# Turning softmax weights on VectorE and ScalarE in place of TensorE, for two pairs of every unit

## The chip, the cores and the metric

The kernel runs on one core of a Trainium2 chip. A core has five engines that run side by side, each through its own list of instructions in order: TensorE (PE, matmuls; its weight loads are shown apart as PEld), VectorE (DVE), ScalarE (ACT), GpSimd (POOL) and SyncE (SP), which issues the transfers (DMA) between DRAM and the on-chip memory SBUF. Matmul results land in eight banks of a second on-chip memory, PSUM. They meet by semaphores. The metric is the device time of one execution, in microseconds (us).

## The reference

Attention inside chunks of 64 positions, and a feed-forward layer behind it, all in float32:

```python
scores = scale * np.matmul(q_c, k_c.transpose(0, 1, 2, 4, 3))     # (8, 8, 9, 64, 64)
scores = scores - np.max(scores, axis=-1, keepdims=True)
attn = np.exp(scores)
attn = attn / (np.sum(attn, axis=-1, keepdims=True) + 1e-09)
out = np.matmul(attn, v_c)
...
x = np.ascontiguousarray(attn_out.transpose(0, 2, 1, 3)).reshape(B, S, H * D)   # 8 x 576 x 512
xn = (x - mu) / np.sqrt(var + 1e-06) * g_ln
ch = np.maximum(xn @ w_ch1, 0.0) @ w_ch2          # 512 to 2048 to 512
return x + ch
```

## The kernel before

The 4608 rows are cut into 18 pairs of 256 rows; nine tiles hold two pairs each. The first three tiles are done by a starting part, in which the weights are also converted. The other six make three units of two tiles, or four pairs. A unit's feed-forward part (`unit_ffn`) is a long row of matmuls on TensorE, in a form with seven products in place of eight. While unit u runs on TensorE, the attention of the four pairs of unit u + 1 is woven in between: so in unit 0 and in unit 1, not in unit 2, and four times in all for the pairs in question (second and fourth).

What sets the order is a table. `attention` is a generator: each `yield` ends a step. `weave` lets the unit's matmuls count a cost (6 for a step of six matmuls, in lines L1109) and runs the next step of a pair once the count reaches the pair's begin (`BEGINS`) plus the step's number in its table (`PAIR_STEPS`). The order on each engine is fixed by this when the program is built; nothing is moved at run time.

The steps of one of these pairs: load q and k; scores by 64 small matmuls (L326); maximum along a row (L333, `top`); scores minus maximum (L359) into `p_sb`, whose 128 partitions hold two chunks' queries and whose 1024 columns hold eight pairs of heads' keys; exponential on ScalarE (L362); the transposed weights `pt_sb`; row sums and their reciprocal (L405 to L407); weights times V (L427); division by the sum (L461); statistics of the rows; normalization on ScalarE (L493); a turn (L500) and sixteen transfers into `rows` (L508), from which `combine` (L811 to L826) builds the next unit's operands in the later part of the unit.

The transposed weights come in three ways. `by_pe` is used in the starting part. In the units, the first and third pair (`STEPS`, `WIDE`) turn 32 x 256 blocks across partitions by sixteen VectorE instructions (L398). The second and fourth (`BY_TENSOR`, `AT_END`) do eight 128 x 128 transposes on TensorE into PSUM (L386) and two copies out by ScalarE (L389).

Beside this ScalarE and VectorE serve the unit's own matmuls. A quarter of the first layer (`q`, 14 steps of six matmuls) uses four PSUM banks, two `a` and two `c`; products with different names accumulate in the same bank one after another, so a copy of a bank's state to `snap` (L1115) or its addition to `hu` (L1118) must be done before the bank is written again: two steps later for the copies of the second and fourth step (index 1 and 3), three or four for the others.

Of the kernel before, what the change touches and what calls it, by code (L numbers as in the profile page):

```python
# [8 lines left out]
F32 = mybir.dt.float32  # L9
# [5 lines left out]
ALU = mybir.AluOpType  # L15
AX = mybir.AxisListType

P = 128
# [7 lines left out]
HP = H // 2  # L26
# [9 lines left out]
LEAD = 3  # L36
# [14 lines left out]

BEGINS = (4, 92, 154, 240)
STEPS = (0, 5, 9, 14, 20, 31, 42, 53, 61, 67, 72, 77, 85, 90, 97, 104, 116, 128, 140)
BY_TENSOR = (-20.9, 6, 11, 18, 33, 37, 40, 48, 54, 60, 67, 72, 80, 86, 98, 110, 122)
WIDE = (-13.9, 5, 9, 14, 22, 35, 48, 61, 69, 75, 80, 85, 93, 98, 105, 110, 122, 134, 146)
AT_END = (-10.9, 6, 11, 18, 33, 37, 40, 48, 54, 62, 72, 77, 84, 92, 104, 116, 128)
PAIR_STEPS = (STEPS, BY_TENSOR, WIDE, AT_END)
SUMS = (392, 402, 414, 545, 563, 578, 590, 602, 604, 616, 628, 640, 658.5, 664, 674)
LATE = (4, 12, 76, 82, 88, 96, 104, 112)
MIXING = ((8, 10, 14, 18, 40, 48, 50, 64), (64, 66, 70, 74, 84, 92, 94, 108))  # L60
# [41 lines left out]
def quad(i):  # L102
    return slice(32 * i, 32 * i + 32)
# [3 lines left out]
def chunk_attention_ffn(ctx: ExitStack, tc: tile.TileContext, qkv, v01, g, g_col, w, out):  # L107
    nc = tc.nc
# [7 lines left out]
    small = ctx.enter_context(tc.tile_pool(name="small", bufs=4))  # L116
# [9 lines left out]
    ident = const.tile([P, P], F32, name="ident")  # L126
# [137 lines left out]
    def sums(pair):  # L264

        if pair not in ys:
            ys[pair] = [ps_y.tile([P, DM], F32, name="y") for _ in range(2)]
        return ys[pair]
# [9 lines left out]
        nc.sync.dma_start(x, spilled[pair])  # L278
        return x

    def attention(pair, xt_cols, xs, by_pe, den_by_pe, rows_of=None, pt_raw=False, pt_by_pe=False):

        moved = pair >= 2 * LEAD + 4
        if pair == 1:
# [13 lines left out]
        groups = 2 * HP  # L298

        def banks():  # L300
            return ps_a.tile([P, 2, DM], F32, name="s")

        def rows(bank):
            return bank.rearrange("p (a d) -> p a d", d=D)

        def halves():

            if den_by_pe:
                assert pair not in taken
                return sums(pair)  # L310
            both = banks()
            return [both[:, j, :] for j in range(2)]
# [7 lines left out]
        for j in range(2):  # L320
            for a in range(HP):
                for h2 in range(2):
                    r = slice(h2 * D, (h2 + 1) * D)
                    for c in range(2):
                        cs = slice(j * P + c * D, j * P + (c + 1) * D)
# [22 lines left out]
        p_sb = work.tile([P, groups, 2, D], F32, name="p_sb", tag="work")  # L348
# [16 lines left out]
        if den_by_pe:  # L365
            nc.gpsimd.memset(v_1.rearrange("p j a b d -> p (j a b) d")[:, :, D:], 1.0)

        if pt_raw:
            pt_sb = raws.tile([P, groups, 2, D], F32, name="pt_raw", tag="wf")
        else:  # L370
            pt_sb = work.tile([P, groups, 2, D], F32, name="pt_sb", tag="work")
        if by_pe:
            pt = halves()
            for a in range(groups):
                cs = slice(a % HP * P, (a % HP + 1) * P)
                nc.tensor.transpose(out=pt[a // HP][:, cs], in_=p_sb[:, a, :, :], identity=ident)  # L376
            for j in range(2):
                nc.scalar.copy(
                    pt_sb[:, j * HP : (j + 1) * HP], pt[j].rearrange("p (a c t) -> p a c t", a=HP, c=2)
                )  # L380
            yield
        elif pt_by_pe:
            pt = halves()
            for a in range(groups):
                cs = slice(a % HP * P, (a % HP + 1) * P)
                nc.tensor.transpose(out=pt[a // HP][:, cs], in_=p_sb[:, a, :, :], identity=ident)  # L386
            yield
            for j in range(2):
                nc.scalar.copy(  # L389
                    pt_sb[:, j * HP : (j + 1) * HP], pt[j].rearrange("p (a c t) -> p a c t", a=HP, c=2)  # L390
                )
            yield
        else:
            for h2 in range(2):
                for j in range(2):
                    for c in range(2):
                        for i in range(2):
                            nc.vector.transpose(  # L398
                                out=pt_sb[quad(2 * h2 + j), :, c, quad(i)], in_=p_sb[quad(2 * c + i), :, h2, quad(j)]
                            )  # L400
                    yield
        den = small.tile([P, groups, 2], F32, name="den")
        rden = small.tile([P, groups, 2], F32, name="rden")
        if not den_by_pe:
            nc.vector.tensor_reduce(out=den, in_=p_sb, axis=AX.X, op=ALU.add)  # L405
            nc.vector.tensor_scalar_add(den, den, 1e-9)
            nc.vector.reciprocal(rden, den)  # L407
            yield

        if by_pe:  # L410
# [9 lines left out]
        for j in range(2):  # L420
            for a in range(HP):
                for h2 in range(2):
                    r = slice(h2 * D, (h2 + 1) * D)
                    ja = j * HP + a
                    for c in range(2):
                        cs = slice(c * D, (c + 1) * D)
# [13 lines left out]
        if den_by_pe:  # L440
# [3 lines left out]
                out=x_j[:, 0], in0=o4[:, :, :, :D], in1=r_b[:, :, :HP].broadcast_to([P, 2, HP, D]), op=ALU.mult  # L444
            )
            for h2 in range(2):
                nc.vector.tensor_tensor(
                    out=x_j[:, 1, h2], in0=o_j[1][h2][:, :, :D], in1=r_b[:, h2, HP:].broadcast_to([P, HP, D]),
                    op=ALU.mult,
                )  # L450
            taken.remove(pair)
        elif by_pe:
            nc.vector.tensor_tensor(
                out=x.rearrange("p j (a b d) -> p b (j a) d", a=HP, b=2),
# [3 lines left out]
        else:  # L458
            x_h = x.rearrange("p j (a b d) -> p (j a) b d", a=HP, b=2)
            for h2 in range(2):  # L460
                nc.vector.tensor_tensor(  # L461
                    out=x_h[:, :, h2, :], in0=rows(o[h2]),
# [22 lines left out]
        if not rows_of:  # L485
            for j in range(2):
                nc.vector.scalar_tensor_tensor(
                    out=xg[:, j, :], in0=x[:, j, :], scalar=mv[:, j, 0:1], in1=g_sb, op0=ALU.subtract, op1=ALU.mult
# [9 lines left out]
        if rows_of and moved:  # L498
            turned = keep.tile([P, 4, 2 * NK, 32], F32, name="x")
            nc.vector.transpose(  # L500
                out=turned.rearrange("p b a t -> p a b t"),
                in_=xg.rearrange("p j (k b f) -> p (j k) b f", k=NK, b=4),
# [281 lines left out]
    def rows_of(i):  # L784
        if "rows" not in shared:
            shared["rows"] = [xtp.tile([P, 2, 2, NK, P], F32, name="rows", tag=f"xt{c}") for c in "hl"]
        return shared["rows"][i // 2][:, i % 2]
# [423 lines left out]
    def play(order, streams):  # L1211
        for c in order:
            next(streams[c])

    xs = {}

    class Tokens:
# [7 lines left out]
                self.x.extend(xtp.tile([P, NK, 2 * PAIR], F32R, name=f"xt{c}") for c in "hl")  # L1225
            return [x[:, :, i * PAIR : (i + n) * PAIR] for x in self.x]

        def attention(self, i, by_pe=False, den_by_pe=False, pt_raw=False, pt_by_pe=False):
            rows = None
            if self.t >= LEAD:  # L1230
                rows = lambda: rows_of((self.t - LEAD) % 2 * 2 + i)
            return attention(2 * self.t + i, lambda: self.cols(i), xs, by_pe, den_by_pe, rows, pt_raw, pt_by_pe)

        def ffn(self, i, n, f0=0, f1=NF, room=()):
            first = 2 * self.t + i
# [2 lines left out]
    tiles = [Tokens(t) for t in range(NTILE)]  # L1238
# [8 lines left out]
    with tc.manual_schedule():  # L1247
        nc.scalar.activation(minus, ident, AF.Copy, scale=-1.0)
        play(START, now)
        now.update(  # L1250
            A=now.pop("E"), B=tiles[2].attention(1), C=tiles[3].attention(0, True), D=tiles[4].attention(0, True),
            G=tiles[3].attention(1), H=tiles[4].attention(1, True, pt_raw=True), S=prepare(), R=start_ring(), T=mix(4, nc.gpsimd, const, "w4"),
            U=mix(5, nc.gpsimd, raws, "raw"), V=mix(6, nc.gpsimd, const, "w8"), a=mix(1, nc.vector, const, "w0"),
            b=mix(2, nc.gpsimd, const, "w1"), c=mix(0, nc.vector, const, "w9", True), d=mix(3, nc.gpsimd, const, "w10", True),
            X=bring(range(2 * LEAD - 2, 2 * LEAD)), P=combine(0, 0), Q=combine(0, 1),
        )
        now.update(zip("u1", tiles[1].ffn(0, 2, room=ROOMS[1])))
        play(layout(ROOMS[1], SECOND), now)
        streams = {}

        def following(u, n):
            n, u = n % 4, u + n // 4
            if (u, n) not in streams and u < UNITS:
                by_pe = len(PAIR_STEPS[n]) == len(BY_TENSOR)
                streams[u, n] = tiles[LEAD + 2 * u + n % 2].attention(n // 2, pt_by_pe=by_pe)
            return streams.get((u, n), iter(" "))

        now["N"] = following(1, 0)
        now.update(zip("u1", tiles[2].ffn(0, 2, room=ROOMS[2])))
        play(layout(ROOMS[2], THIRD, True), now)  # L1270
        side = [(at, now["Q"]) for at in REST]
        for stream, steps in zip((now["d"], mix(NF // 2 - 1, nc.gpsimd, const, "w13")), MIXING):
            side += [(at, stream) for at in steps]
        for u in range(UNITS):
            if u + 1 < UNITS:
                for n in range(4):
                    begin, steps = BEGINS[n], PAIR_STEPS[n]
                    side += [(begin + at, following(u + 1, n)) for at in steps]
                    side.append((begin + steps[0] if n < 3 else NEXT, following(u + 1, n + 1)))
                stream = combine(u + 1)  # L1280
                side += [(at, stream) for at in SUMS]
            side = weave(unit_ffn(u), side)
            if u + 1 < UNITS:
                side += [(at, ending[-1]) for at in LATE]
        assert not side
# [38 lines left out]
```

## Time and profile before

| what | value |
|---|---|
| median of three runs | 819.97 us (817.36 to 820.20) |
| profiled execution, its own time | 818.67 us |
| its span | 816.9 us |
| TensorE busy | 806.0 us, 99% of the span |
| VectorE busy | 609.6 us, 75% |
| ScalarE busy | 363.1 us, 44% |
| GpSimd busy | 183.0 us, 22% |

The span is what the profiler saw between the first and the last instruction; 1.8 us of the execution lie around it. A row such as `357.70 1.09 PE s L386 x8` in the chain means: at 357.70 us eight instructions of line 386 began that write the tile `s`, and 1.09 us passed on the chain. In order of time a row gives start, time until its last instruction ended, engine, line, operation, output <- inputs, shapes, how many, and in brackets the idle time ahead of it and what ended that. Neighbours on VectorE and ScalarE can overlap by some hundredths.

### The profile page before, as it was taken

How to read it: one execution, taken by the hardware profiler on the slowest of the kernel's cores; microseconds unless marked ns; L12 is line 12 of the kernel's file. 1: busy time of each engine (PE TensorE's matmuls, PEld its weight loads, DVE VectorE, ACT ScalarE, POOL GpSimd, SP SyncE). 2: the span in 40 equal slices, each digit the busy share in tenths (PEclk: the TensorE clock that was granted, in tenths of full speed). 3: DMA queues.
4: the chain of work that ended last, by engine and by line, in shares of the span. 5: the costliest groups of instructions: out<-in, count | busy, mean ns of one | idle time of the engine just before them, and what ended most of it. 6: DMA issues, size and time to landing. Idle time of an engine off the chain costs nothing.

```text
span 816.9 us, 15499 instructions
## 1 busy us (share of the span) xinstructions
PE 806.0 (99%) x6170; PEld 680.3 (83%) x6170; DVE 609.6 (75%) x885; ACT 363.1 (44%) x545; POOL 183.0 (22%) x199
## 2 busy tenths in 40 slices
PE   7999999999999999999999999999999999999998
PEld 4888888888888888888888898888888988888887
DVE  6999975787665876869789987697799922249974
ACT  4776432121335434344567442443675522345450
POOL 0111005653857975610100001300000040000000
PEclk9999999999999999999999999999999999999999
DMA  9998315967786239988789578877796678668663
GB/s 359 331 291 243 156 52 183 364 201 253 272 307 252 104 129 367 368 300 302 250 248 329 184 236 307 278 276 257 239 334 213 183 236 252 186 203 285 193 214 108
DMA packets 113928, 201.06 MB, mean 246 GB/s; under 512 B 8512, under 2 KB 75072, under 8 KB 109888
## 3 DMA queue, kind: packets, MB, share of 16 engines
q1 hardware_dynamic: 112560, 195.35, 70.2%
q0 software_dynamic: 1296, 4.72, 3.0%
q8 instruction: 49, 0.80, 0.4%
q14 instruction: 23, 0.19, 0.1%
HBM read 142.89 MB, written 48.23 MB: 234 GB/s over the span
## 4 chain that ended last, share of the span: by engine, by line
PE 98%; DMA 1%; DVE 0%; issue 0%; SPq 0%; ACT 0%
PE y L1109 28%; PE h L589 16%; PE y L613 16%; PE y L1039 12%; PE h L1039 10%; PE s L1039 7%; PE s L326 2%; PE h L427 1%; DMA qk<-qkv 1%; PE s L427 1%; PE s L376 1%; PE s L353 0%; PE s L386 0%; PE y L251 0%; PE s L521 0%; PE y L542 0%
## 5 line engine op out<-in xcount | busy, mean ns | idle before, releaser
L1109 PE MATMUL y<-xc,ring 128*128 128x512 f32 x1008 | 233.4, 391 | 0.0
L1109 PEld LDWEIGHTS y<-xc,ring 128*128 128x128 f32 x1008 | 188.0, 188 | 39.5 <-issue 0.4
L613 PE MATMUL y<-wp,hidden 128*128 128x512 f32 x564 | 137.8, 393 | 0.0
L589 PE MATMUL h<-xth,wp 128*128 128x512 f32 (+1 forms) x432 | 129.6, 371 | 0.0
L613 PEld LDWEIGHTS y<-wp,hidden 128*128 128x128 f32 x564 | 104.4, 188 | 21.4
L1118 DVE TENSOR_TENSOR hu<-y,snap 128x512 f32<-128x512 f32 x72 | 49.2, 685 | 78.7 <-ACT snap L1115 38.3
L589 PEld LDWEIGHTS h<-xth,wp 128*128 128x128 f32 x432 | 78.2, 188 | 14.6 <-DVE hidden L603 0.6
L1039 PE MATMUL y<-ring,hx 128*128 128x512 f32 (+1 forms) x448 | 79.8, 337 | 0.0
L1115 ACT COPY snap<-y 128x512 f32<-128x512 f32 x72 | 41.8, 587 | 83.9 <-PE y L1109 83.8
L935 ACT ACTIVATE hx<-hu 128x1024 fp32r<-128x1024 f32 x61 | 64.3, 1061 | 33.0 <-PE h L1039 24.3
L589 PE MATMUL h<-xtl,wp 128*128 128x512 f32 (+1 forms) x216 | 78.3, 367 | 0.0
L1039 PEld LDWEIGHTS y<-ring,hx 128*128 128x128 f32 x448 | 69.6, 190 | 9.4
L603 DVE SCALAR_TENSOR_TENSOR hidden<-h,hidden 128x512 fp32r<-128x512 f32 (+1 forms) x53 | 33.0, 629 | 54.2 <-ACT hidden L602 54.0
L1039 PE MATMUL h<-ring,hx 128*128 128x256 f32 (+1 forms) x332 | 71.5, 319 | 0.0
L602 ACT ACTIVATE hidden<-h 128x512 fp32r<-128x512 f32 (+1 forms) x53 | 28.5, 545 | 95.5 <-PE h L589 95.5
L944 DVE TENSOR_TENSOR hx<-hu,hx 128x1024 fp32r<-128x1024 f32 x51 | 62.4, 1223 | 7.9 <-ACT hx L935 7.8
L1039 PE MATMUL s<-ring,hx 128*128 128x256 f32 (+1 forms) x236 | 59.7, 335 | 0.0
L997 POOL TENSOR_TENSOR x<-parts,x 128x512 f32<-128x512 f32 x16 | 20.3, 1290 | 169.4 <-DVE x L964 169.0
L1039 PEld LDWEIGHTS h<-ring,hx 128*128 128x128 f32 x332 | 52.0, 190 | 4.8
L398 DVE STREAM_TRANSPOSE pt_sb<-p_sb 32x256 f32<-32x256 f32 x112 | 48.8, 436 | 4.3 <-ACT p_sb L362 2.3
L589 PEld LDWEIGHTS h<-xtl,wp 128*128 128x128 f32 x216 | 40.2, 188 | 6.6 <-ACT xtl L552 0.2
L1039 PEld LDWEIGHTS s<-ring,hx 128*128 128x128 f32 x236 | 40.6, 190 | 4.8
(177 smaller groups left out, 1153.4 us busy)
## 6 DMA issues: line engine op xcount, KB each, us to landing
ring<-wa SPq DMA_DIRECT2D x84, 512.0 KB, 4.6
ring<-wb SPq DMA_DIRECT2D x48, 512.0 KB, 3.7
ring<-w2d SPq DMA_DIRECT2D x36, 512.0 KB, 4.5
raw<-w SPq DMA_DIRECT2D x15, 1024.0 KB, 7.9
out<-x SPq DMA_DIRECT2D x22, 512.0 KB, 5.4
qk<-qkv SPq DMA_DIRECT2D x18, 512.0 KB, 6.4
w2d<-wp SPq DMA_DIRECT2D x16, 512.0 KB, 6.8
wa<-parts SPq DMA_DIRECT2D x32, 256.0 KB, 4.6
```

What stands on the lines that cost most here:

```text
L398: nc.vector.transpose(out=pt_sb[quad(2 * h2 + j), :, c, quad(i)], in_=p_sb[quad(2 * c + i), :, h2, quad(j)])
L589: nc.tensor.matmul(h, lhsT=(wh, wh, wl)[m][:, ks], rhs=(xth, xtl, xth)[m][:, k, :], start=i == 0, stop=i == len(terms) - 1,)
L602: nc.scalar.activation(hh, h, AF.Relu)
L603: nc.vector.scalar_tensor_tensor(out=hl, in0=h, scalar=0.0, in1=hh.bitcast(F32), op0=ALU.max, op1=ALU.subtract)
L613: nc.tensor.matmul(sums(pairs[j // 2])[j % 2], lhsT=(hh, hh, hl)[m], rhs=(wh, wl, wh)[m], start=f == 0 and m == 0, stop=f == NF - 1 and m ...
L935: nc.scalar.activation(hh, self.split[k][2], AF.Relu if x == "1" else AF.Copy)
L944: nc.vector.tensor_tensor(out=hl, in0=x, in1=hh.bitcast(F32), op=ALU.subtract)
L997: engine.tensor_tensor(out=x, in0=self.staged[at][:, 2 * i : 2 * i + 2], in1=x, op=ALU.add)
L1039: nc.tensor.matmul(y, lhsT=(hh, hh, hl, hh)[m], rhs=w.rearrange("p h n -> p (h n)") if m == BOTH else w[:, (0, 1, 0)[m]], start=p == 0 and ...
L1109: nc.tensor.matmul(bank, lhsT=w[:, (0, 0, 1)[m], ks], rhs=x[:, (0, 1, 0)[m], k, :], start=start and k == m == 0, stop=k == 1 and m == 2, s ...
L1115: nc.scalar.copy(out, bank)
L1118: nc.vector.tensor_tensor(out=out, in0=bank, in1=s, op=ALU.add)
```

## The change

The second and fourth pair of each unit no longer go to TensorE for the transposed weights. VectorE first sums the rows (`weigh`, the three instructions that stood behind the transposes before), then turns all 32 x 32 blocks of `p_sb` where they stand, in one instruction of 128 x 1024 (L380 of the new file). Then sixteen ScalarE copies of 32 partitions x 256 elements (L401) bring the blocks to their partitions in `pt_sb`, four in each step. The step tables of both pairs are new: the steps up to the copies come earlier in the unit, and in the fourth pair L427 and all behind it come later.

```diff
-BY_TENSOR = (-20.9, 6, 11, 18, 33, 37, 40, 48, 54, 60, 67, 72, 80, 86, 98, 110, 122)
+BY_SCALAR = (-20.9, -6, 0, 5, 10, 14, 20, 25, 30, 35, 48, 54, 60, 67, 72, 80, 86, 98, 110, 122)
...
+        def weigh():
+            nc.vector.tensor_reduce(out=den, in_=p_sb, axis=AX.X, op=ALU.add)
+            nc.vector.tensor_scalar_add(den, den, 1e-9)
+            nc.vector.reciprocal(rden, den)
+
+        if by_scalar:
+            weigh()
+            yield
+            both = p_sb.rearrange("p a h (b t) -> p a (h b) t", t=32)
+            nc.vector.transpose(out=both, in_=both)
+            yield
...
-        elif pt_by_pe:
-            pt = halves()
-            for a in range(groups):
-                cs = slice(a % HP * P, (a % HP + 1) * P)
-                nc.tensor.transpose(out=pt[a // HP][:, cs], in_=p_sb[:, a, :, :], identity=ident)
-            yield
-            for j in range(2):
-                nc.scalar.copy(
-                    pt_sb[:, j * HP : (j + 1) * HP], pt[j].rearrange("p (a c t) -> p a c t", a=HP, c=2)
-                )
-            yield
+        elif by_scalar:
+            for c in range(2):
+                for i in range(2):
+                    for h2 in range(2):
+                        for j in range(2):
+                            nc.scalar.copy(
+                                pt_sb[quad(2 * h2 + j), :, c, quad(i)], p_sb[quad(2 * c + i), :, h2, quad(j)]
+                            )
+                    yield
```

`AT_END` changes in the same way. Line numbers behind the change are 8 higher in the new file (L1117 for L1109, L1123 for L1115, L1126 for L1118, L435 for L427, L508 for L500).

ScalarE's list at the second pair, unit 0, before:

```order
L493 ACTIVATE xg<-x,vare,rstd 128x512 x2
L1115 COPY snap<-y 128x512 x2
L362 ACTIVATE p_sb<-p_sb 128x1024
L1115 COPY snap<-y 128x512 x3
L389 COPY pt_sb<-s 128x512 x2
L1115 COPY snap<-y 128x512
L1123 ACTIVATE hu<-hu 128x512
```

and after:

```order
L501 ACTIVATE xg<-x,vare,rstd 128x512 x2
L1123 COPY snap<-y 128x512
L362 ACTIVATE p_sb<-p_sb 128x1024
L1123 COPY snap<-y 128x512
L401 COPY pt_sb<-p_sb 32x8x32 x4
L1123 COPY snap<-y 128x512
L401 COPY pt_sb<-p_sb 32x8x32 x4
L1123 COPY snap<-y 128x512
L401 COPY pt_sb<-p_sb 32x8x32 x4
L1123 COPY snap<-y 128x512
L401 COPY pt_sb<-p_sb 32x8x32 x4
L1123 COPY snap<-y 128x512
```

Three of the six snap copies now stand between the four groups of block copies, and the exponential has moved ahead of one snap.

ScalarE's list at the fourth pair, unit 0, before:

```order
L362 ACTIVATE p_sb<-p_sb 128x1024
L1115 COPY snap<-y 128x512 x2
L389 COPY pt_sb<-s 128x512 x2
L1115 COPY snap<-y 128x512 x4
L935 ACTIVATE hx<-hu 128x1024
```

and after:

```order
L362 ACTIVATE p_sb<-p_sb 128x1024
L1123 COPY snap<-y 128x512
L401 COPY pt_sb<-p_sb 32x8x32 x8
L1123 COPY snap<-y 128x512
L401 COPY pt_sb<-p_sb 32x8x32 x4
L1123 COPY snap<-y 128x512
L401 COPY pt_sb<-p_sb 32x8x32 x4
L1123 COPY snap<-y 128x512 x3
L943 ACTIVATE hx<-hu 128x1024
```

Eight block copies now stand ahead of the second snap copy, which serves the `a` bank of the second half.

TensorE's list at the fourth pair, unit 0, before:

```order
L326 MATMUL s<-qk 64x64 x32
L1109 MATMUL y<-xc,ring 128x512 x42
L386 MATMUL s<-ident,p_sb 128x128 x8
L1109 MATMUL y<-xc,ring 128x512 x12
L427 MATMUL h<-v_t,pt_sb 64x64 x32
L1109 MATMUL y<-xc,ring 128x512 x48
```

and after:

```order
L326 MATMUL s<-qk 64x64 x32
L1117 MATMUL y<-xc,ring 128x512 x66
L435 MATMUL h<-v_t,pt_sb 64x64 x32
L1117 MATMUL y<-xc,ring 128x512 x36
```

The transposes are gone, and L427 comes twelve matmuls, two steps, later. At the second pair only the transposes go: L427 keeps its place behind the same 18 matmuls. (For the 32 of L326 and of L427 in such a list the trace shows 64 entries.)

VectorE's list at the second pair, unit 0, after (before, L500 stood between L333 and L359, and L405 to L407 behind two L1118 and L1126):

```order
L333 TENSOR_REDUCE top<-s 128x16
L359 TENSOR_TENSOR p_sb<-s,top 128x2x8x64
L1126 TENSOR_TENSOR hu<-y,snap 128x512
L508 STREAM_TRANSPOSE x<-xg 128x8x4x32
L372 TENSOR_REDUCE den<-p_sb 128x16
L373 TENSOR_SCALAR den<-den 128x16
L374 RECIPROCAL rden<-den 128x16
L380 STREAM_TRANSPOSE p_sb<-p_sb 128x1024
L1126 TENSOR_TENSOR hu<-y,snap 128x512
L1134 SCALAR_TENSOR_TENSOR hu<-hu 128x1024
```

Sum and turn now stand ahead of the second of these L1126, and top and subtraction ahead of the first.

More of the change, by code (lines that the diff above doesn't have):

```diff
@@ L53 @@
 STEPS = (0, 5, 9, 14, 20, 31, 42, 53, 61, 67, 72, 77, 85, 90, 97, 104, 116, 128, 140)
-BY_TENSOR = (-20.9, 6, 11, 18, 33, 37, 40, 48, 54, 60, 67, 72, 80, 86, 98, 110, 122)
+BY_SCALAR = (-20.9, -6, 0, 5, 10, 14, 20, 25, 30, 35, 48, 54, 60, 67, 72, 80, 86, 98, 110, 122)
 WIDE = (-13.9, 5, 9, 14, 22, 35, 48, 61, 69, 75, 80, 85, 93, 98, 105, 110, 122, 134, 146)
-AT_END = (-10.9, 6, 11, 18, 33, 37, 40, 48, 54, 62, 72, 77, 84, 92, 104, 116, 128)
-PAIR_STEPS = (STEPS, BY_TENSOR, WIDE, AT_END)
+AT_END = (-10.9, 2, 8, 14, 19, 24, 31, 36, 41, 46, 57, 63, 69, 79, 84, 91, 99, 110, 121, 132)
+PAIR_STEPS = (STEPS, BY_SCALAR, WIDE, AT_END)
 SUMS = (392, 402, 414, 545, 563, 578, 590, 602, 604, 616, 628, 640, 658.5, 664, 674)
@@ L279, in unspill, with attention @@
         return x
-    def attention(pair, xt_cols, xs, by_pe, den_by_pe, rows_of=None, pt_raw=False, pt_by_pe=False):
+    def attention(pair, xt_cols, xs, by_pe, den_by_pe, rows_of=None, pt_raw=False, by_scalar=False):
         moved = pair >= 2 * LEAD + 4
@@ L366, in attention @@
             nc.gpsimd.memset(v_1.rearrange("p j a b d -> p (j a b) d")[:, :, D:], 1.0)
+        den = small.tile([P, groups, 2], F32, name="den")
+        rden = small.tile([P, groups, 2], F32, name="rden")
+        def weigh():
[8 more added lines that the diff above has]
+            yield
         if pt_raw:
@@ L401, in attention @@
                     yield
[L402 to L407, printed above, removed]
+        if not den_by_pe and not by_scalar:
+            weigh()
             yield
@@ L1226, in cols, with attention @@
             return [x[:, :, i * PAIR : (i + n) * PAIR] for x in self.x]
-        def attention(self, i, by_pe=False, den_by_pe=False, pt_raw=False, pt_by_pe=False):
+        def attention(self, i, by_pe=False, den_by_pe=False, pt_raw=False, by_scalar=False):
             rows = None
@@ L1231, in attention @@
                 rows = lambda: rows_of((self.t - LEAD) % 2 * 2 + i)
-            return attention(2 * self.t + i, lambda: self.cols(i), xs, by_pe, den_by_pe, rows, pt_raw, pt_by_pe)
+            return attention(2 * self.t + i, lambda: self.cols(i), xs, by_pe, den_by_pe, rows, pt_raw, by_scalar)
         def ffn(self, i, n, f0=0, f1=NF, room=()):
@@ L1263, in following @@
             if (u, n) not in streams and u < UNITS:
-                by_pe = len(PAIR_STEPS[n]) == len(BY_TENSOR)
-                streams[u, n] = tiles[LEAD + 2 * u + n % 2].attention(n // 2, pt_by_pe=by_pe)
+                streams[u, n] = tiles[LEAD + 2 * u + n % 2].attention(n // 2, by_scalar=n % 2 == 1)
             return streams.get((u, n), iter(" "))
```

## Prediction

> **What bounds the kernel.** I read the page's busy times and its chain, then the waits by TensorE (PE in the rows), then the chain in order of time around the removed instructions, and last ScalarE (ACT) and VectorE (DVE) in order of time at those places.
>
> ```profile
> PE 806.0 (99%) x6170; PEld 680.3 (83%) x6170; DVE 609.6 (75%) x885; ACT 363.1 (44%) x545; POOL 183.0 (22%) x199
> PE 98%; DMA 1%; DVE 0%; issue 0%; SPq 0%; ACT 0%
> ```
>
> TensorE is the bound almost alone. So an instruction taken from it is worth its time on the chain, and one given to another engine is free until a matmul waits for it. The rows of the chain (start, us, what) at the four places of L386, and one step of six matmuls for scale:
>
> ```profile
> 357.70 1.09 PE s L386 x8
> 358.79 4.11 PE y L1109 x18
> 362.90 1.09 PE h L427 x64
> ...
> 397.33 0.87 PE s L386 x8
> 398.21 2.74 PE y L1109 x12
> 400.94 1.09 PE h L427 x64
> ...
> 507.98 1.36 PE y L1109 x6
> ...
> 524.59 0.87 PE s L386 x8
> 525.47 4.09 PE y L1109 x18
> 529.56 1.09 PE h L427 x64
> ...
> 564.31 0.87 PE s L386 x8
> 565.19 2.73 PE y L1109 x12
> 567.92 1.09 PE h L427 x64
> ```
>
> The reader sees no gap: L427, the product of weights and V, starts as soon as the matmuls ahead are done.
>
> **The gain.** Four groups of eight transposes go: 1.09 + 3 x 0.87 = 3.70 us, and no row beside them changes by more than 0.02. The whole of it is 0.45% of 818.67, so even a perfect result is inside the 0.5% that a measurement of this kernel can tell from no change. The two evacuating copies per pair (L389) also go, but ScalarE gets sixteen copies instead, and L427 must wait for the last of them. So the question is when these end.
>
> **The price of a copy.** Each moves 32 partitions x 256 elements. The trace of before has no such copy on ScalarE. The nearest rows:
>
> ```profile
> 801.53 1.20 ACT L969 COPY x<-y 128x256 f32<-128x256 f32 x4 [5.12 <-PE y L1039]
> 413.67 2.95 ACT L935 ACTIVATE hx<-hu 128x1024 fp32r<-128x1024 f32 x3
> 347.85 1.13 ACT L1088 CAST mixed<-mixed 128x512 fp32r<-128x512 f32 x2
> 357.55 1.54 ACT L1115 COPY snap<-y 128x512 f32<-128x512 f32 x3
> 335.72 3.62 DVE L398 STREAM_TRANSPOSE pt_sb<-p_sb 32x256 f32<-32x256 f32 x8
> L969 ACT COPY x<-y 128x256 f32<-128x256 f32 x12 | 3.6, 386 | 9.7 <-PE y L1039 9.7
> L935 ACT ACTIVATE hx<-hu 128x1024 fp32r<-128x1024 f32 x61 | 64.3, 1061 | 33.0 <-PE h L1039 24.3 <-PE y L1039 8.7
> L398 DVE STREAM_TRANSPOSE pt_sb<-p_sb 32x256 f32<-32x256 f32 x112 | 48.8, 436 | 4.3 <-ACT p_sb L362 2.3
> ```
>
> Copies of the same length from PSUM follow each other every (1.20 - 0.39) / 3 = 0.27 us, though one lasts 0.39: they overlap. From SBUF 1024 elements come every (2.95 - 1.06) / 2 = 0.945, and two of 512 in 1.13, about 0.51 apart with 0.62 for one; on that line 256 come every 0.945 - 3/2 x (0.945 - 0.51) = 0.29. I take 0.30 between starts and 0.40 for one. Below is 0.27. Above stands the VectorE row, which does the same move of 32 x 256 between partition groups: eight in 3.62, one every (3.62 - 0.44) / 7 = 0.455 against 0.436 for one. There nothing overlaps. For ScalarE that would be 0.42 a copy. I take the row of the same engine, and keep the other as a rival. The Trainium skill, "ScalarE: Activation LUTs", section What ACT_TABLE_LOAD costs, gives 186 ns + 0.833 ns per element with about 93 ns of overlap: 306 ns here, against the 270 of the PSUM row; by it the sum below would be about 0.4 us more. A PSUM evacuation (L1115) takes (1.54 - 0.59) / 2, about 0.49, in a queue.
>
> **When the copies can start.** VectorE must first add up and then turn p_sb in place. The rows that set this, second pair (units 0 and 1):
>
> ```profile
> 351.81 0.56 ACT L1115 COPY snap<-y 128x512 f32<-128x512 f32 x1
> 352.47 0.69 DVE L1118 TENSOR_TENSOR hu<-y,snap 128x512 f32<-128x512 f32 x1 [3.45 <-DMA qk<-qkv]
> 353.08 1.22 DVE L333 TENSOR_REDUCE top<-s 128x16 f32<-128x1024 f32 x1
> 354.21 1.24 DVE L500 STREAM_TRANSPOSE x<-xg 128x1024 f32<-128x1024 f32 x1
> 355.37 1.19 DVE L359 TENSOR_TENSOR p_sb<-s,top 128x1024 f32<-128x1024 f32 x1
> ...
> 398.65 1.21 DVE L405 TENSOR_REDUCE den<-p_sb 128x16 f32<-128x1024 f32 x1
> ...
> 400.28 1.16 DVE L1126 SCALAR_TENSOR_TENSOR hu<-hu 128x1024 f32<-128x1024 f32 x1
> ...
> 517.83 0.59 ACT L1115 COPY snap<-y 128x512 f32<-128x512 f32 x1 [0.25 <-PE y L1109]
> 518.45 0.69 DVE L1118 TENSOR_TENSOR hu<-y,snap 128x512 f32<-128x512 f32 x1 [3.76 <-ACT snap L1115]
> ```
>
> In the new order VectorE does top and the subtraction ahead of this L1118, and behind it L500, sum, reciprocal and the turn. The exponential stands behind the snap copy and is ready by 353.4. So in unit 0: L500 at 353.08; sum at 354.24 (L500 holds the queue 355.37 - 354.21 = 1.16); the turn 400.28 - 398.65 = 1.63 later, at 355.87; priced like L500, 1.24, it ends at 357.11. This is new VectorE work, and its cover is VectorE's idle 25%; the next L1118 behind it ends at about 357.7, just when TensorE needs that bank.
>
> *Second pair, unit 0.* The copies start at 357.16 (0.05 for a release). In ScalarE's queue stand four copies, a snap, and so on, three snaps in between: 16 x 0.30 + 3 x 0.49 = 6.27; the last copy ends 0.10 after that, and L427 starts at 357.16 + 6.27 + 0.10 + 0.05 = 363.58. TensorE would be there at 357.70 + 4.09 = 361.8: it waits 1.8 us, where it saved 1.1. Against 362.90 of before: **+0.68**.
>
> *Second pair, unit 1.* The same chain from 518.45: turn done at 523.08, L427 at 529.55, against 529.56: **0.0**.
>
> *Fourth pair.* Here eight copies stand ahead of the snap of the second bank, which the step of six matmuls two steps later needs. Rows:
>
> ```profile
> 393.30 1.25 DVE L500 STREAM_TRANSPOSE x<-xg 128x1024 f32<-128x1024 f32 x1
> 393.64 1.05 ACT L362 ACTIVATE p_sb<-p_sb 128x1024 f32<-128x1024 f32 x1
> 397.43 0.59 ACT L1115 COPY snap<-y 128x512 f32<-128x512 f32 x1 [2.14 <-PE y L1109]
> 560.68 1.05 ACT L362 ACTIVATE p_sb<-p_sb 128x1024 f32<-128x1024 f32 x1
> ```
>
> The exponential ends at 394.69, so sum at 394.74, turn 396.37 to 397.61, copies from 397.66. The snap that ran at 397.43 now starts at 397.66 + 8 x 0.30 = 400.06 and ends at 400.65; its step could start at 397.33 + 2 x 1.36 = 400.06, so TensorE waits 0.64. Then four copies, snap, four copies: last end 403.54, L427 at 403.59. L427 stands two steps later than before: 400.94 + 2 x 1.36 = 403.66. Net **-0.07**. Unit 1, by 560.68: **-0.03**.
>
> Sum: +0.68 + 0.0 - 0.07 - 0.03 = **+0.6 us**. The gain of 3.7 is taken back by four waits of 0.8 to 1.8 us. The profiled execution took 818.67 (span 816.9 and 1.8 around it), so 819.3. The median of the runs shown is 819.97, 1.3 above the profiled one; they spread from 817.36 to 820.20.
>
> *Other moves.* Behind the fourth pair's later L427 everything of that pair moves some 2 us: its sums, L493, L500, and sixteen transfers to rows (L508) on SP, each set now one ring load later.
>
> ```profile
> 592.36 2.50 SPq L508 DMA_DIRECT2D rows<-x  x4
> DMA to landing us min/median/max: 2.6/2.8/3.0
> 597.38 1.34 ACT L826 ACTIVATE rows<-rows,mhalf 128x512 f32<-128x512 f32 x2
> ```
>
> The last of them (issued at 594.3) lands at 597.3 and its reader L826 starts at 597.38. Two us later, ScalarE would wait there. I cost it at nothing, since ScalarE waits for TensorE in this stage anyhow (L935's 33.0 us of idle time); without that cover it is up to 2 us in each of two units.
>
> **Rivals.**
> 1. *The copies don't overlap* (slower). A move between partition groups makes ScalarE finish one instruction before the next, as the VectorE row shows: 0.42 a copy and 0.61 a snap. Then the same sums give L427 at 365.74, 531.71, 405.63 and 572.66: +2.84, +2.15, +1.97, +2.01, in all +9.0, 827.7 us (1.1%). It decides from about 0.36 us a copy on, where the sum passes 4.1 us. For it: the same transfer on VectorE, where the 128-partition L1118 and L333 do overlap (0.69 lasting, 0.61 apart). Against: no ScalarE row shows a hold. The Trainium skill, "VectorE: DVE Perf Modes", section Two Vector instructions with no wait between them, has this as a rule for VectorE: an instruction whose start quadrant differs from the one before waits until that has finished; L398's 0.455 agrees; of ScalarE it says nothing.
> 2. *The copies are cheap.* A quarter of the partitions, or a turn that ends earlier, lets every copy end before TensorE asks: 818.67 - 3.7 = 815.0. For it only that no row shows the operation; L398 against L500 (0.44 for 256, 1.24 for 1024) shows that fewer partitions make VectorE no faster.
> 3. *The late rows of the fourth pair* cost what I cover: +0.6 and 2 to 4 us, 821 to 823.
>
> **Chances.** Forecast 0.60, rival 1 0.28, rival 2 0.06, rival 3 0.06. At 0.27 a copy the forecast's sum is -1.1 (817.5), at 0.32 it is +1.9 (820.5); with the spread of the runs its own range is 816.5 to 822. The whole range must take in rival 1, which alone holds more than 2 in 10: 816.5 to 829. Slower by over 0.5%: rival 1 and half of 3, 0.31. Faster by over 0.5%: 0.03, since the gain can't reach it unaided. Within 0.5%: 0.66.
>
> **What would show it.** Right: no L386; four stretches in which TensorE waits for ScalarE's pt_sb or snap, together 3 to 5 us; the turn at about 1.24 us; groups of four copies in 1.3 us. Wrong towards rival 1: four copies in 1.7 us and waits of 13 us in all. Towards rival 2: L427 without a wait. Rival 3: ScalarE idle ahead of L826 for the transfers, and TensorE idle in the same place. The forecast also falls if the turn in place takes other than L500's 1.24, since all sixteen copies stand behind it.

## Result, and the profile after

| kernel | median | runs | ratio to before, 95% interval | span of the profiled execution |
|---|---|---|---|---|
| before | 819.87 us | 4 | | 816.9 us |
| changed | 827.46 us (826.87 to 829.45) | 4 | 1.0104 [1.0077, 1.0130] | 825.1 us (own time 827.06) |

The change makes the kernel 1.0% slower: 7.6 us by the medians, 8.2 us by the spans. That is the time of the first rival (827.7 us), not that of the forecast (819.3 us).

The page of the changed kernel, busy times and chain:

```profile
PE 806.1 (98%) x6138; PEld 677.9 (82%) x6138; DVE 613.6 (74%) x889; ACT 384.5 (47%) x601; POOL 184.7 (22%) x199
PE 84%; DVE 7%; ACT 5%; DMA 3%; issue 1%; POOL 0%; SPq 0%; ACTq 0%; DVEq 0%
```

TensorE has 32 instructions less, and yet is busy as long as before (806.0). VectorE and ScalarE, which were not on the chain, now hold 12% of it: not of lost time, but of the stretches in which the chain runs over the work that TensorE waits for. TensorE's waits, whole run, longest sums first (waited for; us in total, times, longest):

```profile
PE y L1117 <- ACT snap L1123: 4.4, 4, 1.6
PE h L435 <- ACT pt_sb L401: 4.4, 6, 1.2
```

Both lines are new, 8.8 us in ten waits. TensorE in order of time, second pair of unit 0:

```profile
355.74 5.37 PE L1117 MATMUL y<-xc,ring 128*128 128x512 f32 x20
361.75 1.66 PE L1117 MATMUL y<-xc,ring 128*128 128x512 f32 x6 [0.63 <-ACT snap L1123]
363.33 0.33 PE L435 MATMUL h<-v_t,pt_sb 64*64 64x64 f32 x2
364.84 0.33 PE L435 MATMUL h<-v_t,pt_sb 64*64 64x64 f32 x4 [1.18 <-ACT pt_sb L401]
365.68 1.08 PE L435 MATMUL h<-v_t,pt_sb 64*64 64x64 f32 x57 [0.51 <-ACT pt_sb L401]
```

It stops first for an evacuation, then twice inside L435, whose first products need one copy each. A group that ends before a wait also looks longer, since no next matmul overlaps its last one: six matmuls of a step take 1.66 here, against 1.36 from row to row before. So, as an estimate, ten waits hide some 10 x 0.3 = 3 us more in the busy time. With the 8.8 us listed that is 11.8, and 3.70 of gain + 8.2 of loss makes 11.9.

ScalarE at the same place:

```profile
357.14 1.65 ACT L401 COPY pt_sb<-p_sb 32x256 f32<-32x256 f32 x4 [2.82 <-DVE p_sb L380]
358.82 0.59 ACT L1123 COPY snap<-y 128x512 f32<-128x512 f32 x1
359.43 1.65 ACT L401 COPY pt_sb<-p_sb 32x256 f32<-32x256 f32 x4
...
363.97 1.65 ACT L401 COPY pt_sb<-p_sb 32x256 f32<-32x256 f32 x4
```

One copy lasts 0.403 us (median of 64), and four take 1.65: one starts (1.65 - 0.403) / 3 = 0.416 us after the other. Nothing overlaps. The evacuation between two groups doesn't either: from its start to the next copy 0.61. And in the fourth pair, where eight copies stand ahead of the snap that the next step needs, ScalarE and then TensorE:

```profile
400.46 3.31 ACT L401 COPY pt_sb<-p_sb 32x256 f32<-32x256 f32 x8 [2.35 <-DVE p_sb L380]
403.80 0.59 ACT L1123 COPY snap<-y 128x512 f32<-128x512 f32 x1
...
404.44 3.06 PE L1117 MATMUL y<-xc,ring 128*128 128x512 f32 x12 [1.56 <-ACT snap L1123]
...
408.38 1.14 PE L435 MATMUL h<-v_t,pt_sb 64*64 64x64 f32 x58 [0.51 <-ACT pt_sb L401]
```

The evacuation ends at 404.39 and TensorE starts 0.05 later. So the copies cost 0.416, where the forecast took 0.30. Why, and whether that is the whole of it, is what the experiments ask.

### The profile page after: what moved, and what is told of

The parts are those of the page before. It is cut to its first block, busy times and chain, and to the rows that moved or that the text cites. A ratio compares the mean times of both kernels' runs of the same rounds, so it can differ in the third digit from the quotient of the medians.

```text
span 825.1 us, 15489 instructions
## 1 busy us (share of the span) xinstructions
PE 806.1 (98%) x6138; PEld 677.9 (82%) x6138; DVE 613.6 (74%) x889; ACT 384.5 (47%) x601; POOL 184.7 (22%) x199
## 4 chain that ended last, share of the span: by engine, by line
PE 84%; DVE 7%; ACT 5%; DMA 3%; issue 1%; POOL 0%; SPq 0%; ACTq 0%; DVEq 0%
PE y L1117 19%; PE y L621 15%; PE h L597 15%; PE y L1047 12%; PE h L1047 10%; PE s L1047 7%; ACT pt_sb L401 3%; PE s L326 2%; PE h L435 1%; DMA ring<-wa 1%; DMA wp<-wfs 1%; DMA qk<-qkv 1%; ACT snap L1123 1%; DVE stats L479 1%; DVE den L372 1%
## 5 line engine op out<-in xcount | busy, mean ns | idle before, releaser
L1117 PE MATMUL y<-xc,ring 128*128 128x512 f32 x1008 | 233.9, 391 | 4.6 <-ACT snap L1123 4.4
L1117 PEld LDWEIGHTS y<-xc,ring 128*128 128x128 f32 x1008 | 187.8, 188 | 46.3 <-ACT snap L1123 7.0
L1126 DVE TENSOR_TENSOR hu<-y,snap 128x512 f32<-128x512 f32 x72 | 48.9, 684 | 75.1 <-ACT snap L1123 43.9
L1123 ACT COPY snap<-y 128x512 f32<-128x512 f32 x72 | 41.7, 587 | 69.0 <-PE y L1117 68.7
```

The costliest lines, as they stand in the source:

```text
L1117: nc.tensor.matmul(bank, lhsT=w[:, (0, 0, 1)[m], ks], rhs=x[:, (0, 1, 0)[m], k, :], start=start and k == m == 0, stop=k == 1 and m == 2, s ...
L1123: nc.scalar.copy(out, bank)
L1126: nc.vector.tensor_tensor(out=out, in0=bank, in1=s, op=ALU.add)
```

## Experiments

The theory from here on: ScalarE starts an instruction before the one ahead has finished (0.31 apart for these copies) only if it starts in the same group of 32 partitions, in its input and in its output; else it waits for the end (0.416). The rivals: a copy on 32 partitions costs 0.416 whatever its groups are; or the form of its rows does it; or the loss comes from elsewhere (the turn, the order, the late rows).

**No change of group.** Every copy reads partitions 0 to 31 and writes partitions 0 to 31, each of a step at its own columns; the move to other partitions is left out, so the blocks are not the right ones. So that `pt_sb` is written everywhere, the turn writes into it out of place. Instructions, sizes and order stay.

```diff
-            nc.vector.transpose(out=both, in_=both)
+            pt_sb = work.tile([P, groups, 2, D], F32, name="pt_sb", tag="work")
+            nc.vector.transpose(out=pt_sb.rearrange("p a h (b t) -> p a (h b) t", t=32), in_=both)
...
-                                pt_sb[quad(2 * h2 + j), :, c, quad(i)], p_sb[quad(2 * c + i), :, h2, quad(j)]
+                                pt_sb[quad(0), :, h2, quad(j)], p_sb[quad(0), :, h2, quad(j)]
```

> All sixteen copies at all four places from partitions 0-31 to 0-31, each of a step's four to a place of its own; the blocks are wrong. Theory 'changed start group holds, and this spacing is what the prediction mis-sized': 0.31 us a copy, 0.48 a snap, and the prediction's sum with 0.31, +1.0 to +1.5 us, 820 to 821 us, 1.001 to 1.002 of before. Rival 'the loss is elsewhere': spacing 0.31, time 825 to 827. Rivals by partitions or pattern: spacing 0.416, time 827.5.

Measured: 820.14 us, ratio 1.0008 [0.9994, 1.0023] with 10 runs, span 817.4 us. ScalarE in order of time, the second pair of unit 0:

```profile
357.25 1.33 ACT L402 COPY pt_sb<-p_sb 32x256 f32<-32x256 f32 x4 [2.82 <-DVE pt_sb L381]
358.49 0.57 ACT L1124 COPY snap<-y 128x512 f32<-128x512 f32 x1
358.96 1.32 ACT L402 COPY pt_sb<-p_sb 32x256 f32<-32x256 f32 x4
```

and TensorE at both places:

```profile
363.13 0.32 PE L436 MATMUL h<-v_t,pt_sb 64*64 64x64 f32 x2 [0.66 <-ACT pt_sb L402]
363.75 1.10 PE L436 MATMUL h<-v_t,pt_sb 64*64 64x64 f32 x59 [0.29 <-ACT pt_sb L402]
...
401.62 3.02 PE L1118 MATMUL y<-xc,ring 128*128 128x512 f32 x12 [0.67 <-ACT snap L1124]
404.57 1.16 PE L436 MATMUL h<-v_t,pt_sb 64*64 64x64 f32 x64
```

Copies of the same shape now start (1.33 - 0.403) / 3 = 0.31 apart, and a group overlaps the snap on either side (358.49 is before 357.25 + 1.33; 0.47 from the snap to the next copy). With that alone, nearly all of the loss is gone. The forecast said L427 at 363.58 in unit 0, a wait of 0.64 for the snap in the fourth pair, and +0.6 in all; here it is 363.75, 0.67, and 817.4 - 816.9 = +0.5. So the forecast's other terms hold, and the rivals of shape, turn and order fall.

**One group changed, the other not.** At each of the four places the copies have other groups: second pair of unit 0 none changed; fourth pair of unit 0 all 128 partitions; second pair of unit 1 the output group changes; fourth pair of unit 1 the input group. The turn writes into `pt_sb` as above.

```diff
...
-                            nc.scalar.copy(
-                                pt_sb[quad(2 * h2 + j), :, c, quad(i)], p_sb[quad(2 * c + i), :, h2, quad(j)]
-                            )
+                            of, to, place = quad(0), quad(0), (h2, quad(j))
+                            if pair == 13:
+                                of = to = slice(0, P)
+                            if pair == 16:
+                                to, place = quad(2 * h2 + j), (c, quad(i))
+                            if pair == 17:
+                                of = quad((2 * h2 + j + 2 * c + i) % 4)
+                            nc.scalar.copy(pt_sb[to, :, place[0], place[1]], p_sb[of, :, h2, quad(j)])
```

> As the first mixed kernel, but the copies of a step that keep their output group now write four different places, so that none has to wait for an earlier copy to the same place (they did there: starts 0.437 apart, and 0.31 where no such wait stood). Second pair, unit 0: partitions 0-31 to 0-31. Fourth, unit 0: all 128 to themselves. Second, unit 1: 0-31 to a changing group. Fourth, unit 1: a changing group to 0-31. Blocks are wrong again. Theory 'a changed start group holds the next instruction': 0.31, 0.31, 0.416, 0.416 us between starts in a step; if only the output's group counts, 0.31 at the last. Rival 'fewer than 128 partitions': 0.416, 0.31, 0.416, 0.416. Rival 'pattern': 0.416 at all four.

Measured (one run): 823.31 us, span 821.3. ScalarE in order of time, the four places:

```profile
357.55 1.33 ACT L409 COPY pt_sb<-p_sb 32x256 f32<-32x256 f32 x4 [2.82 <-DVE pt_sb L381]
...
398.88 2.56 ACT L409 COPY pt_sb<-p_sb 128x256 f32<-128x256 f32 x8 [2.35 <-DVE pt_sb L381]
...
524.07 1.66 ACT L409 COPY pt_sb<-p_sb 32x256 f32<-32x256 f32 x4 [2.27 <-DVE pt_sb L381]
525.75 0.59 ACT L1129 COPY snap<-y 128x512 f32<-128x512 f32 x1
526.23 1.64 ACT L409 COPY pt_sb<-p_sb 32x256 f32<-32x256 f32 x4
...
567.08 3.40 ACT L409 COPY pt_sb<-p_sb 32x256 f32<-32x256 f32 x8 [2.40 <-DVE pt_sb L381]
570.39 0.57 ACT L1129 COPY snap<-y 128x512 f32<-128x512 f32 x1
570.98 1.70 ACT L409 COPY pt_sb<-p_sb 32x256 f32<-32x256 f32 x4
572.59 0.57 ACT L1129 COPY snap<-y 128x512 f32<-128x512 f32 x1
```

Spacings with 0.40 for one: 0.31 with 32 partitions and 0.31 with 128, (1.66 - 0.40) / 3 = 0.42 where the output group changes, (3.40 - 0.40) / 7 = 0.43 where the input group does. Either change alone holds. The evacuations tell more. They read PSUM and write `snap`, from partition 0 on. At 525.75 the copy ahead had written group 3: the snap starts at its end (524.07 + 1.66). The copy behind the snap starts in group 0 as the snap did, and follows after 0.48, overlapping, though the snap covers all four groups: it is the group of the first partition that counts. At 570.39 and 572.59 the copy ahead had written group 0, and the snap starts 0.09 before its end, at 572.59 although that copy had read SBUF in group 1 and the snap reads PSUM in group 0. So an input is not held for another group in the other memory. At 570.98 the copy behind the snap reads another group than the copy ahead of it, and waits out the snap (0.59). Whether a read of PSUM changes the group remembered for SBUF isn't shown: every copy of this experiment that changes its input right behind a snap reads another group than the last copy and than the snap. As far as these rows go, this is the rule that the Trainium skill, "VectorE: DVE Perf Modes", section Two Vector instructions with no wait between them, gives for VectorE, with one remembered start group for the input and one for the output of each memory. These rows show it on ScalarE, for copies.

**The other order of the loops.** If only one of the two groups counted, writing one output group's four blocks in a row would keep it fixed within a step. The computation is the same.

```diff
-            for c in range(2):
-                for i in range(2):
-                    for h2 in range(2):
-                        for j in range(2):
+            for h2 in range(2):
+                for j in range(2):
+                    for c in range(2):
+                        for i in range(2):
```

> The right blocks in another order: the four copies of a step write one partition group and read four. If only a change of the output's group holds: three of four starts 0.31 apart, 16 copies in about 5.4 us where they took 6.7, 821.5 to 823 us. If a change of either group holds: 0.416 and 827.5 us, as the changed kernel.

Measured: 828.41 us, ratio 1.0108 [1.0078, 1.0138], span 827.4. ScalarE in order of time, the second pair of unit 0:

```profile
358.19 1.65 ACT L401 COPY pt_sb<-p_sb 32x256 f32<-32x256 f32 x4 [2.82 <-DVE p_sb L380]
359.75 0.57 ACT L1123 COPY snap<-y 128x512 f32<-128x512 f32 x1
```

Steps of four still take 1.65, eight take 3.31; TensorE's waits are those of the changed kernel (4.4 and 4.4). The input changes at every copy, and that is enough. (The first step writes group 0 and ends with a read of group 3, and the snap again starts 0.09 before its end. The span is longer than the changed kernel's 825.1 by other things: a wait of 1.1 for a transfer early on, and a granted clock of 0.50 from 367 to 370.) Each of the sixteen blocks has its own pair of groups, so no order of them avoids the hold.

**Two controls that missed.** These came first, and tell less. In the first all copies stay within one group, but the four of a step have the same output columns:

```diff
...
-                                pt_sb[quad(2 * h2 + j), :, c, quad(i)], p_sb[quad(2 * c + i), :, h2, quad(j)]
+                                pt_sb[quad(0), :, c, quad(i)], p_sb[quad(0), :, h2, quad(j)]
```

> All sixteen copies at all four places go from partitions 0-31 to partitions 0-31, so the blocks are wrong, but their number, length and order stay (VectorE turns p_sb into pt_sb, not in place). Theory 'changed start group holds': 0.30 us a copy and the sum of the prediction, 819.3 us, 0.990 of the changed kernel's 827.5 and 0.999 of the kernel before. Rivals by partitions or pattern: 0.416 a copy and 827.5 us. If the loss had another cause than the copies' spacing (late rows transfers, the turn on VectorE), the spacing would fall to 0.30 and the time stay near 827.

Measured: 827.83 us, ratio 1.0113 [1.0090, 1.0136]. The time seems to speak for the rivals by partitions or pattern. ScalarE's rows in order of time show another cause:

```profile
356.59 1.72 ACT L402 COPY pt_sb<-p_sb 32x256 f32<-32x256 f32 x4 [2.82 <-DVE pt_sb L381]
358.21 0.57 ACT L1124 COPY snap<-y 128x512 f32<-128x512 f32 x1
```

Four copies take 1.72, (1.72 - 0.40) / 3 = 0.44 apart and so more than in the changed kernel, but the snap overlaps the last of them (358.21 is before 356.59 + 1.72). Each copy overwrote what the one before had written, and so waited for it; by what means, a semaphore for instance, the views don't show. The control had put in a wait of its own in place of the one it took away. Part of its time is something else again: in the profiled execution the granted clock was near 0.50 for some 3 us from 365 and from 536, where the changed kernel has 1.00 at both places. The second has the four places of the mixed experiment, with the same fault where the output group is fixed:

```diff
...
+                            to, of = {
+                                12: (quad(0), quad(0)), 13: (slice(0, P), slice(0, P)),
+                                16: (quad(2 * h2 + j), quad(0)), 17: (quad(0), quad((2 * h2 + j + 2 * c + i) % 4)),
+                            }[pair]
+                            nc.scalar.copy(pt_sb[to, :, c, quad(i)], p_sb[of, :, h2, quad(j)])
```

> Wrong blocks are copied, so that four kinds of copy stand at the four places, with the same 256 elements in the same pattern (VectorE turns p_sb into pt_sb, not in place, so that all of pt_sb is written). Second pair, unit 0: partitions 0-31 to 0-31 always. Fourth pair, unit 0: all 128 partitions to themselves. Second pair, unit 1: 0-31 to a group that changes with each copy. Fourth pair, unit 1: a group that changes to 0-31. Theory 'a changed start group holds the next instruction': starts 0.30 us apart at the first two places, 0.416 at the last two (0.30 at one of these if only the input or only the output counts). Rival 'fewer than 128 partitions don't overlap': 0.416, 0.30, 0.416, 0.416. Rival 'the pattern of 32-element runs, or source and target tile, prevent overlap': 0.416 at all four.

Measured (one run): 826.5 us, span 824.7. Only the second pair of unit 1, whose copies don't overwrite each other, could be read: four in 1.66 with a changing output group, 0.42 apart. Where all copies had 128 partitions they were 0.44 apart inside a step and 0.31 across its end: the wait again.

**The two pairs apart.** In each kernel one of the two pairs goes back to TensorE's transposes and its old table, the other keeps the change. For the second pair alone:

```diff
-AT_END = (-10.9, 2, 8, 14, 19, 24, 31, 36, 41, 46, 57, 63, 69, 79, 84, 91, 99, 110, 121, 132)
+AT_END = (-10.9, 6, 11, 18, 33, 37, 40, 48, 54, 62, 72, 77, 84, 92, 104, 116, 128)
...
```

> Only the second pair is changed; the fourth goes to TensorE as before, with its old step table. Theory 'each place pays its own wait for the copies': the second pair's two places keep their +2.8 and +2.1 us, the fourth's +1.9 and +1.9 go: 819.9 + 4.9 = 824.8 us, 1.006 of before. Rival 'the later rows transfers of the fourth pair cost': all or most of the 7.6 us goes, 820 to 821 us.

Measured: 825.40 us, ratio 1.0078 [1.0063, 1.0093], span 823.4. TensorE's waits in it, whole run:

```profile
PE h L448 <- ACT pt_sb L414: 3.4, 4, 1.2
PE y L1130 <- ACT snap L1136: 1.3, 2, 0.6
```

And for the fourth pair alone:

```diff
-BY_SCALAR = (-20.9, -6, 0, 5, 10, 14, 20, 25, 30, 35, 48, 54, 60, 67, 72, 80, 86, 98, 110, 122)
+BY_SCALAR = (-20.9, 6, 11, 18, 33, 37, 40, 48, 54, 60, 67, 72, 80, 86, 98, 110, 122)
...
```

> The second pair goes back to TensorE's transposes; only the fourth pair has the turn and the copies, with the places of the change. Theory (each pair's late L427 is a delay of its own, added to those before it): the fourth pairs lost 1.88 and 1.9 us in the changed kernel, so 819.9 + 3.8 = 823.7 us, and no wait for copies at the second pair. Rival (the second pair's delays set off a later part of the fourth's, or the other way round; the parts do not add up): the change cost 7.6 us and the second pair alone 5.5 us, so only 2.1 are left, 822.0 us.

Measured: 822.50 us, ratio 1.0042 [1.0027, 1.0056], span 820.1. The same view:

```profile
PE y L1130 <- ACT snap L1136: 3.2, 2, 1.6
PE h L448 <- ACT pt_sb L414: 1.0, 2, 0.5
```

The waits add up to 0.1 us: 3.4 + 1.0 = 4.4 for the copies, 1.3 + 3.2 = 4.5 for the evacuations, against 4.4 and 4.4 together. The times do so within their spread: alone the two cost 0.78% and 0.42%, in sum 1.2%, or 9.8 us with some 1.7 either way, against 8.5 [6.3, 10.7] for the change. The fourth pair's loss, 2.2 to 4.6 us by its interval, holds the 3.8 of the theory and just leaves out the 2.1 of the rival. In the profile of the second pair alone some of its 6.5 us are not the change's. Before unit 0 began 0.7 were lost: TensorE had waited 1.0 for a transfer (`wp`, at 48.83), a wait that the list of the kernel before doesn't have. About 1.5 went behind the second pair of unit 1, from 535 on (1.1 in L448 and L328, 0.4 in the ninety matmuls after them, against the changed kernel): the granted clock was 0.69 in the first microsecond and 0.50 in the next two, where the kernel before and the changed one have 1.00 at this place. What lowered it there isn't shown. That leaves 4.3 for the two waits, near the 2.78 and 1.70 read below.

**Half of the copies on GpSimd.** The two with j = 1 in each step go to GpSimd; all else is the changed kernel, and the computation is whole.

```diff
-                            nc.scalar.copy(
-                                pt_sb[quad(2 * h2 + j), :, c, quad(i)], p_sb[quad(2 * c + i), :, h2, quad(j)]
-                            )
+                            copy = nc.scalar.copy if j == 0 else nc.gpsimd.tensor_copy
+                            copy(pt_sb[quad(2 * h2 + j), :, c, quad(i)], p_sb[quad(2 * c + i), :, h2, quad(j)])
```

> Eight of the sixteen copies (those with j = 1) go to GpSimd, in turn with ScalarE's eight. Theory 'L427 waits for the last copy and the snap for the copies ahead': ScalarE's eight end at about 362.3 in the second pair of unit 0, 0.5 us late, so GpSimd's price decides: at 0.45 us a copy all waits are under 0.6 us and the time is about 817; at 0.75 (between GpSimd's 0.20 for 2 elements and 1.29 for 512) about 820; at 1.0 about 828. Rival 'the waits come from VectorE's turn or from the transfers': no change from 827.5 whatever GpSimd does.

Measured: 816.32 us, ratio 0.9964 [0.9940, 0.9987]. Once more, in more rounds:

> The kernel in which GpSimd does every other copy, once more in more rounds. Theory: all sixteen copies of a pair end before TensorE asks, so the gain of the eight transposes, 3.7 us in all, shows less what else moved: 816 to 817 us, ratio 0.995 to 0.998. Rival: the first result (816.32 us) was the lucky end of the spread: no difference from before, 819 to 820 us.

Measured: 815.96 us (814.62 to 817.21, 11 runs), ratio 0.9960 [0.9946, 0.9974], span 813.7. In order of time, the second pair of unit 0 on ScalarE, GpSimd and TensorE:

```profile
357.50 0.82 ACT L402 COPY pt_sb<-p_sb 32x256 f32<-32x256 f32 x2 [2.82 <-DVE p_sb L380]
357.59 4.45 POOL L402 COPY pt_sb<-p_sb 32x256 f32<-32x256 f32 x8 [4.33 <-DVE p_sb L380]
...
361.85 0.83 ACT L402 COPY pt_sb<-p_sb 32x256 f32<-32x256 f32 x2
...
362.35 1.52 PE L434 MATMUL h<-v_t,pt_sb 64*64 64x64 f32 x63
```

GpSimd's eight end at 362.04, ScalarE's eight at 362.68, and TensorE starts the product at 362.35 with the blocks that are there; the list of its matmuls' waits names no evacuation any more. Of the 3.70 us of removed transposes, 3.2 come out (816.9 - 813.7). This version is 0.4% faster than the kernel before, and so faster than the changed one. Its time is near that of the second rival (815.0), but not for that rival's reason: the copies are not cheap, they are shared.

## Why the prediction was wrong

- **What bounds the kernel**: right. TensorE's own work was the chain, and the question was only when the last copy ends.
- **The gain**: right, 3.70 us. The eight transposes are gone at all four places, and where the copies don't hold TensorE up 3.2 of it shows. That so small a gain couldn't be told from no change was too strict: with 11 runs against 21 its interval, 0.9946 to 0.9974, leaves out 1.
- **The start of the copies**: right to 0.03 at three of the four places, once the delays that had come before are taken off; the second pair of unit 1 is 0.42 early, by the gap of 0.44 named below. In unit 0 the turn was to start at 355.87 and end at 357.11; VectorE in order of time:

```profile
354.27 1.18 DVE L372 TENSOR_REDUCE den<-p_sb 128x16 f32<-128x1024 f32 x1
...
355.87 1.19 DVE L380 STREAM_TRANSPOSE p_sb<-p_sb 128x1024 f32<-128x1024 f32 x1
```

  It took 1.19 in place of 1.24, and the first copy began at 357.14 (forecast 357.16).
- **The price of a copy**: this is the step that failed. The prediction took 0.30 us between starts from ScalarE's rows of 128 partitions, and the chip gave 0.416; a snap between them took 0.61, not 0.49. The duration of one was right (0.403 against 0.40). In the rows chosen every instruction starts at partition 0, so they could not show what a change of group does. The only row of a move between groups, VectorE's L398, was given to the rival for being on another engine. It was the nearer one: like the copies, it changes groups at each instruction.
- **The sum**: with 0.42 and 0.61 the same working gives +2.84, +2.15, +1.97, +2.01 for the four places. To read them in the changed kernel, its chain in order of time, L435 and the products of the pair before it:

```profile
365.68 1.08 PE h L435 x57
388.38 1.10 PE h L435 x64
408.38 1.14 PE h L435 x58
514.10 1.09 PE h L435 x64
536.02 1.08 PE h L435 x57
558.72 1.16 PE h L435 x64
578.77 1.14 PE h L435 x58
```

  Second pair, unit 0: 365.68 - 362.90 = 2.78. Fourth: the third pair's product is now 388.38 - 385.56 = 2.82 late, and 408.38 - (400.94 + 2.72 for two steps) - 2.82 = 1.90. Unit 1: 514.10 - 509.34 = 4.76 late; second pair 536.02 - 529.56 - 4.76 = 1.70; fourth 578.77 - (567.92 + 2.72) - (558.72 - 552.53) = 1.94. In all 8.3, where the spans show 8.2 and the rival had 9.0. What is short is mostly unit 1's second pair. The changed kernel did not repeat there a gap of 0.44 that the profiled execution of before had:

```profile
511.80 0.33 PE L326 MATMUL s<-qk 64*64 64x64 f32 x2 [0.44 <-issue]
```

  Counted without this gap its loss is 2.14, as the rival had it (2.15).
- **What would show it**: the signs were well chosen for the groups of copies (1.65 against 1.3 and 1.7). Of the rival's 13 us of waits the list shows 8.8 only; 11.9 were lost, and the rest is in the matmuls that look longer ahead of a wait.
- **Rival 2** (cheap copies) and **rival 3** (late rows) did not happen. In the later part of unit 1, ScalarE in order of time in the changed kernel:

```profile
604.62 1.05 ACT L819 CAST xc<-rows 128x1024 fp32r<-128x1024 f32 x1
605.79 1.34 ACT L834 ACTIVATE rows<-rows,mhalf 128x512 f32<-128x512 f32 x2
```

and before:

```profile
596.44 1.04 ACT L811 CAST xc<-rows 128x1024 fp32r<-128x1024 f32 x1
```

  The reader of the late rows starts 1.17 behind the cast ahead of it, where it was 0.94 (597.38). That is 0.2 us, and ScalarE's waits for TensorE take it in, so costing it at nothing was right.
- **The chances**: the rival's point of decision (0.36 us a copy) lay halfway between the two rows. A doubt between 0.30 and 0.42 should have been weighed nearer to even than 0.60 to 0.28.

## What to carry to other kernels

When an operation isn't in the trace, choose the row that is like it in what it does between instructions (here: changing partition groups), ahead of the row from the same engine. Small ScalarE copies that change partition groups at every step had no overlap here (0.416 apart, 0.403 each); count them at their full duration, and the evacuations among them too. Work taken from a saturated TensorE pays only if its substitute ends before TensorE asks, so split a serial run of small copies over two idle engines before giving it to one. And a control that overwrites its own output puts in the wait that it should take away.

## What was not expected of the hardware

- ScalarE holds a copy back when its input or output starts in another group of partitions than the last one used in that memory: 0.42 to 0.43 us between copies that last 0.40, against 0.31 without. A snap that follows such a copy or precedes it is held by the same condition (0.61 to the next copy, against 0.48). Other instructions than copies were not tried.
- GpSimd does such a copy in 0.395 us (median of 32), and eight of them in 4.45, since some took up to 1.38; what made those longer was not tried. (The profile's times for GpSimd are rough.)
- Copies that overwrite each other run 0.44 apart on ScalarE, also with no change of group; the hold makes it 0.42.
